# A fused attention and gated-MLP kernel on one core: S2 asked for amid the keys, first keys projected in halves, 256 tokens' features turned by TensorE, batch 0's k v 128 columns wide, steps in a new order

## The chip, the cores and the metric

One core of one Trainium2 chip runs the kernel. The core has five engines with a queue of instructions each: TensorE (PE in the profile, with its weight loads as PEld), VectorE (DVE), ScalarE (ACT), GpSimd (POOL) and SyncE (SP), which here only issues DMAs. An engine takes its instructions in order and waits on semaphores where it needs another's result. The metric is the time of one execution in microseconds; lower is better.

## The reference

Inputs q, k, v have 4 batches, 4 heads, 1088 tokens and 32 dims. Two 8 x 32 sketches S1, S2 give each token 64 features, the products of 8 and 8. The attention is linear: keys and values are summed into a 64 x 32 matrix per head, and each query reads it.

```python
def phi(x):
    a = np.einsum('rd,bhsd->bhsr', S1, x)
    b = np.einsum('rd,bhsd->bhsr', S2, x)
    return np.einsum('bhsi,bhsj->bhsij', a, b).reshape(*x.shape[:-1], r * r)
q_p, k_p = (phi(q), phi(k))
kv = np.einsum('bhsf,bhsd->bhfd', k_p, v)
z = np.sum(k_p, axis=2)
num = np.einsum('bhsf,bhfd->bhsd', q_p, kv)
den = np.einsum('bhsf,bhf->bhs', q_p, z)[..., None] + 1e-06
x = (num / den)            # then 4352 tokens x 128
h = x @ w_in               # 128 x 2048
g = h * (1.0 / (1.0 + np.exp(-beta * h)))
out = g @ w_out            # 2048 x 128
```

## The kernel before

The order of all steps is written out by hand in the string SEQ (L809). Each word of it is a key of the table DO and emits one small step; an engine's queue holds its instructions in the order of these words. Engines run apart from each other and meet on semaphores only.

Per batch, the steps are these. `tk` and `tq` (L433, L439) turn k and q in 32 x 32 blocks on DVE. `kp` (L446) multiplies k by both sketches on PE into a bank `kps`; it has two halves, one for each half of the turned k. `ka` (L464) turns that back into `kab`, the two sets of 8 factors of each token. `o` (L598) forms 64 features `kp` of each key by an outer product, on DVE or POOL, in five parts. `kv` (L627) sums features times v over the nine token groups into the bank `kvz`: for each group and head one product whose weights are 32 columns of v and whose moving operand is 64 features. `gr`, `gc`, `wh`, `wc` (L475 to L505) form from `kab` a small product `wq`, so that the projection of q, step `q` (L510), gives its factors and the summands of its denominator together. `dm`, `di`, `da`, `dx` (L544 to L586) sum the denominator, invert it and scale one factor. `p` (L606) forms q's features `qo`, `t` (L618) turns them in 32 x 32 blocks on DVE into `qt`, `n` (L681) multiplies them by `nd`, a turned copy of `kvz`, with 32 small products for a batch part, and `x` (L698) casts the result into `xT`, 128 features by tokens.

Batch 0 has its queries in two parts: A, the first 256 tokens, and C, the rest. For batch 0, `nd` is made by `ns`, `nt`, `nc` (L642 to L663): a copy of `kvz` repeated four times, two transposes on PE, and a copy. For the other batches `nf` and `ng` (L665, L669) turn it on DVE and pass it through DRAM.

The second half of the work goes over chunks of tokens, 256, 256, seven of 512, and 256. `W` (L395) is a wave: the products of four (or two) of the 16 blocks of w_in with `xT` into a two-bank buffer `wave`, of which there are two, and one Silu on ACT that empties it into `g`. `V` (L424) is a second product of a wave's `g` with the blocks of w_out into the bank `moeout`; after a chunk's last one DVE turns the sum and SP stores it. `kvz` of batch 0 has the bank of the first `moeout`. There are 68 waves and 68 second products.

The weights are prepared on the way. `be` and `bc` (L290, L302) spread beta over the partitions, by PE into a bank and by a copy; `wi` (L308) scales a quarter of w_in by beta; `wa`, `wv`, `wg` (L329, L336) scale one of 16 blocks of w_out by 1/beta on ACT, DVE and POOL. `z0` (L717) writes one element of w_out's tile, so that its load starts only then. `m2` and `ms` (L281, L273) make masked copies of the sketches. Steps `e`, `h`, `i`, `mW` (L248) are filler products on PE with no result.

Loads go through SP's queue, in the order `lk0.0`, `lk0.1` (halves of batch 0's k), `lqA`, `lv0`, `lqC`, the four quarters of w_in, and so on; S1 and beta are issued by ACT, S2 and a second copy of beta by POOL.

## Time and profile before

| | us |
|---|---|
| median of three runs | 102.17 |
| lowest and highest run | 101.83, 102.18 |
| the profiled execution | 100.9 |
| its span, first to last instruction | 99.1 |
| last product on PE ends | 95.2 |
| PE idle from the end of the products to the end of the span | 3.9 |

The profile is one execution. A row of the order-of-time view has the start, the time from the first to the end of the last of the instructions merged into it, the engine, the line, the operation, the tiles, the form and the count; in brackets, the engine's idle time before it and who ended it. A row of the stretches view has, after the stretch and its length, the busy time and count of PE, PEld, DVE, ACT and POOL, then PE's granted clock, the DMA share and GB/s. Busy time of PE counts a product from start to modelled end, so overlapping products make it busy without making it full. The granted clock is 1.00 in the mean of the whole span.

### The profile page before, as it was taken

To read this page: it belongs to the slowest core of one execution; us is meant where nothing else is said; L and a number is where in the kernel's file an instruction comes from. 1 tells how busy PE (TensorE), PEld (TensorE's weight loads), DVE (VectorE), ACT (ScalarE), POOL (GpSimd) and SP (SyncE) were. 2 spreads that over 40 slices of the span, in tenths; PEclk is the share of its full clock that TensorE was granted. 3 is DMA by queue.
4 is the path that set the end of the run, shared out by engine and by line. 5 is a ranking of instruction groups with operands and counts; after the bars stand their busy time and mean duration, and the time that the engine had idled before them with its cause. 6 is when DMAs were issued, how large, how long until landed. Compare 5 with 4: busy or idle time off the path is not lost.

```text
span 99.1 us, 3150 instructions
## 1 busy us (share of the span) xinstructions
PE 92.4 (93%) x1302; PEld 48.7 (49%) x1302; DVE 58.1 (59%) x128; ACT 76.7 (77%) x102; POOL 36.1 (36%) x58
## 2 busy tenths in 40 slices
PE   5989998997999999999999999999999999999940
PEld 2525536665867544434445444444444444446720
DVE  3569989888579998449998335699630020020210
ACT  0505299984869797997998897999989999999910
POOL 5739989998594900077370000320000000000000
PEclk9999999999999999999999999999999999999999
DMA  2999999914971320058043141215015006014163
GB/s 55 273 351 317 395 370 388 270 42 107 387 225 38 62 44 7 0 149 307 17 95 67 20 76 30 53 31 83 2 20 85 1 2 104 7 20 70 17 100 59
DMA packets 24031, 11.75 MB, mean 119 GB/s; under 512 B 19245, under 2 KB 21837, under 8 KB 24017
## 3 DMA queue, kind: packets, MB, share of 16 engines
q1 hardware_dynamic: 23256, 11.44, 41.8%
q8 instruction: 10, 0.16, 0.6%
q10 hardware_dynamic: 696, 0.09, 0.6%
q0 software_dynamic: 64, 0.02, 0.4%
q14 instruction: 5, 0.03, 0.1%
HBM read 9.22 MB, written 2.33 MB: 117 GB/s over the span
## 4 chain that ended last, share of the span: by engine, by line
PE 63%; POOL 12%; ACT 9%; DMA 5%; SPq 4%; issue 2%; DVE 0%; POOLq 0%; ACTq 0%
PE wave L407 27%; PE moeout L379 26%; ACT g L415 8%; DMA w_in_sb<-in_moe_w_in_dram 5%; POOL winp L311 5%; PE nps L689 5%; PE kvz L632 4%; POOL qo L591 3%; POOL kp L591 3%; SPq L143 2%; SPq L164 1%; PE qps L518 1%; ACT xT L705 1%; PE kps L456 1%; SPq L178 1%
## 5 line engine op out<-in xcount | busy, mean ns | idle before, releaser
L415 ACT ACTIVATE g<-wave 128x1024 f16<-128x1024 f32 x68 | 64.8, 1027 | 7.0 <-PE wave L407 6.8
L407 PE MATMUL wave<-xT,winp 128*128 128x512 f16 (+1 forms) x160 | 39.7, 348 | 0.8 <-issue 0.4
L379 PE MATMUL moeout<-g,woutp 128*128 128x512 f16 (+1 forms) x160 | 37.6, 347 | 0.0
L407 PEld LDWEIGHTS <-winp 128*128 128x128 f16 x160 | 17.0, 114 | 16.7 <-issue 6.4
L379 PEld LDWEIGHTS <-woutp 128*128 128x128 f16 x160 | 15.4, 97 | 12.5
L591 POOL TENSOR_TENSOR kp<-kab 128x512 f32<-128x512 f32 (+1 forms) x17 | 16.1, 981 | 10.8 <-DVE kab L465 10.8
L389 DVE STREAM_TRANSPOSE o_sb<-moeout 128x512 f32<-128x512 f32 (+1 forms) x10 | 6.3, 631 | 22.0 <-PE moeout L379 22.0
L622 DVE STREAM_TRANSPOSE qt<-qo 128x512 f32<-128x512 f32 (+1 forms) x21 | 11.8, 605 | 0.2
L591 POOL TENSOR_TENSOR qo<-qa,qab 128x512 f32<-128x512 f32 (+1 forms) x11 | 9.5, 886 | 5.3 <-DVE qa L570 5.3
L535 DVE STREAM_TRANSPOSE qab<-qps 128x576 f32<-128x576 f32 (+2 forms) x10 | 6.0, 642 | 2.1 <-PE qps L518 2.0
L689 PE MATMUL nps<-qt,nd 32*32 32x288 f32 (+2 forms) x320 | 7.0, 364 | 0.1
L253 PE MATMUL kvz<-idle 128*128 128x384 f16 (+1 forms) x21 | 5.1, 399 | 1.1 <-DVE idle L215 1.1
L632 PE MATMUL kvz<-kp,v 128*32 128x64 f32 x288 | 5.7, 222 | 0.3 <-POOL kp L591 0.3
L434 DVE STREAM_TRANSPOSE kT<-k 128x544 f32<-128x544 f32 x8 | 5.6, 719 | 0.4 <-DMA k<-in_k_dram 0.3
L547 POOL TENSOR_TENSOR tmp<-qab 128x64 f32<-128x64 f32 (+2 forms) x3 | 1.8, 589 | 11.0 <-DVE qab L535 11.0
L440 DVE STREAM_TRANSPOSE qT<-q 128x576 f32<-128x576 f32 (+3 forms) x8 | 5.8, 721 | 0.0
L253 PEld LDWEIGHTS <-idle 128*128 128x128 f16 x36 | 3.5, 110 | 4.6 <-issue 2.3
L632 PEld LDWEIGHTS kvz<-kp,v 128*32 128x32 f32 x288 | 4.4, 109 | 2.6 <-issue 1.6
L465 DVE STREAM_TRANSPOSE kab<-kps 128x288 f32<-128x288 f32 x8 | 3.6, 464 | 3.2 <-PE kps L456 3.2
L689 PEld LDWEIGHTS nps<-qt,nd 32*32 32x32 f32 x320 | 3.9, 103 | 2.7 <-DVE qt L622 0.5
L311 POOL TENSOR_TENSOR winp<-w_in_sb,beta_bc 128x512 f16<-128x512 f32 x4 | 5.1, 1274 | 0.1
L332 ACT ACTIVATE woutp<-w_out_sb,rbeta 128x128 f16<-128x128 f32 x15 | 5.0, 399 | 0.1
(63 smaller groups left out, 54.8 us busy)
## 6 DMA issues: line engine op xcount, KB each, us to landing
k<-in_k_dram SPq DMA_DIRECT2D x3, 544.0 KB
q<-in_q_dram SPq DMA_DIRECT2D x3, 544.0 KB, 5.1
v<-in_v_dram SPq DMA_DIRECT2D x4, 288.0 KB
v<-in_v_dram SPq DMA_DIRECT2D x4, 256.0 KB, 5.8
w_in_sb<-in_moe_w_in_dram SPq DMA_DIRECT2D x4, 256.0 KB, 5.4
w_out_sb<-in_moe_w_out_dram SPq DMA_DIRECT2D x4, 256.0 KB, 5.7
out_dram<-o_sb SPq DMA_DIRECT2D x16, 64.0 KB, 3.6
k<-in_k_dram SPq DMA_DIRECT2D x2, 272.0 KB, 2.9
```

Source lines behind the costliest of these rows:

```text
L253: nc.tensor.matmul(out=t[:, P : P + cols], lhsT=idle, rhs=cut(idle, [[0, cols // P], [1, P]]), start=fresh or other, stop=True, skip_group ...
L311: eng.tensor_tensor(out=winp[:, n].rearrange("p c u -> p (c u)"), in0=w_in_sb[:, o : o + FQ], in1=beta_bc[:, o : o + FQ], op=MUL,)
L379: nc.tensor.matmul(out=moe["acc"][:, :tw], lhsT=woutp[:, j // U, j % U, :], rhs=g[jj], start=(j == 0), stop=(j == NJ - 1),)
L389: nc.vector.transpose(out=o_sb[:, :nt, :].rearrange("p t d -> p (t d)"), in_=moe["acc"][:, :tw])
L407: nc.tensor.matmul(out=wv[:, jj // per, o : o + tw], lhsT=winp[:, j // U, :, j % U], rhs=xT[:, t0 : t0 + tw], start=True, stop=True,)
L415: nc.scalar.activation(out=g, in_=wv, func=ACTF.Silu)
L440: nc.vector.transpose(out=qT2[b % 2][:, t0:t1].rearrange("p t s -> p (t s)"), in_=q_t[b][:, t0:t1].rearrange("p t d -> p (t d)"),)
L535: nc.vector.transpose(out=cut(QAB[nm], [[32, 2], [32 * H, n], [1, 32]], 64 * i), in_=PS["qps", nm][i][:, :, : 32 * n],)
L591: eng.tensor_tensor(out=cut(o, [[F, n], [R, R], [1, R]]), in0=cut(a, [[sa, n], [1, R], [0, R]]), in1=cut(b_, [[sb_, n], [0, R], [1, R]]), ...
L622: nc.vector.transpose(out=QT[nm][:, j0:j1].rearrange("p j h c s -> p (j h c s)"), in_=QO[nm][:, j0:j1].rearrange("p j h f -> p (j h f)"),)
L632: nc.tensor.matmul(out=PS["kvz", b][32 * h : 32 * h + 32, :F], lhsT=v_t[b][:, h, j, :], rhs=KP[b][:, j, h, :], start=(j == 0), stop=(j == ...
L689: nc.tensor.matmul(out=t[g // 2][32 * h : 32 * h + 32, g % 2, : 32 * n], lhsT=ND[b][rows, h, fc, :], rhs=QT[nm][rows, :, h, fc, :], start= ...
```

## The change

S2's load is issued by SP (`ls1s`) between the two halves of k, no longer by POOL. The first keys are projected in two halves (`kz0`, `ky0`). Batch 0's `kv` takes, for each of nine groups, two products whose weights are the 128 features of two heads and whose moving operand is 64 columns of v of the same two heads; each sum holds the blocks of both heads with both, of which the equal ones are used. A copy `nn` of 128 columns of it into `ndA` takes the place of `ns`. Part A's features are turned by PE: `TA` makes 128 x 128 transposes, `uA` copies them, and `nA` makes four products of 256 tokens; `xA` copies one block of 128 tokens each. `nd` for part C comes from `nt`, 16 products with slices of the identity, and `nc`. Filler steps `i` are four times three products of 128 columns. Scaling of the second quarter of w_in (`wi1D`) and the product `dmC` go from POOL to DVE, two blocks of w_out (`wg8`, `wg9`) go to POOL, and one beta copy (`bc01D`) to DVE. `store` gets an argument that halves its transfers; it is 0 in every call. SEQ has a new order.

```diff
-    def keep_warm(n, cols, fresh=False, other=False):
-        if other and "warm" not in PS:
-            PS["warm"] = one("warm")
-        t = PS["warm"] if other else kvz0
+    def keep_warm(n, cols, fresh=False, at=P):
         for _ in range(n):
             nc.tensor.matmul(
-                out=t[:, P : P + cols],
+                out=kvz0[:, at : at + cols],
...
         for j in range(j0, j1):
+            if b == 0:
+                for c in range(2):
+                    nc.tensor.matmul(
+                        out=PS["kvz", b][:, F * c : F * c + F],
+                        lhsT=KP[b][:, j, 2 * c : 2 * c + 2, :].rearrange("p h f -> p (h f)"),
+                        rhs=v_t[b][:, 2 * c : 2 * c + 2, j, :],
+                        start=(j == 0 and c == 0),
+                        stop=(j == NJK - 1),
+                        skip_group_check=True,
+                    )
+                continue
...
+    def nd_pairs(copy):
+        t = PS["ndA"] = sbA.tile([P, 2, 2, 32], F32, tag="ndA", name="ndA", bufs=1)
+        copy(out=t.rearrange("p c n d -> p (c n d)"), in_=kvz0[:, :P])
+    def nd_turn():
+        for n in range(4):
+            for g in range(4):
+                nc.tensor.matmul(
+                    out=kvz0[32 * g : 32 * g + 32, P + 64 * n : P + 64 * n + 64],
+                    lhsT=ident[:, 32 * n : 32 * n + 32],
+                    rhs=PS["ndA"][:, :, n // 2, :],
...
+    def turn_a(j):
+        if j == 0:
+            PS["A"] = one("uA")
+            QT["A"] = sbA.tile([P, 2, 2, P], F32, tag="qtA", name="qt", bufs=1)
+        for c in range(2):
             nc.tensor.matmul(
...
+                out=PS["A"][:, 2 * P * j + P * c : 2 * P * j + P * c + P],
+                lhsT=QO["A"][:, j, 2 * c : 2 * c + 2, :].rearrange("p h f -> p (h f)"),
                 rhs=ident,
                 is_transpose=True,
...
+    def copy_a(j, copy):
+        copy(out=QT["A"][:, :, j, :], in_=cut(PS["A"], [[P, 2], [1, P]], 2 * P * j))
+    def num_a():
+        for h in range(H):
+            rows = slice(F * (h % 2), F * (h % 2) + F)
+            nc.tensor.matmul(
+                out=PS["A"][32 * h : 32 * h + 32, : 2 * P],
+                lhsT=PS["ndA"][rows, h // 2, h % 2, :],
+                rhs=QT["A"][rows, h // 2].rearrange("p j s -> p (j s)"),
...
+    def put_xa(i, copy):
+        copy(out=xT[:, P * i : P * i + P], in_=PS["A"][:, P * i : P * i + P])
...
-    DO["i"] = lambda: keep_warm(1, 384, other=True)
+    DO["i"] = lambda: keep_warm(3, P, at=3 * P)
...
-        ls0a ls1g lk0.0s lk0.1s lb4a lbpg m lqAs lv0s lqCs li0s li1s li2s li3s mW h h h h e e tk00 ts msP m2P
-        sq1P sq0P tk01 kp0t ka00 ka01 tqA be00 be01 kx0A bc00A bc01A gr0 gc0D h h wh0 wc0A z0 lo0s lk1s lo1s
-        lo2s lo3s h h qAww o00D rb o01D qtA0 qtA1 tqC lq1s lv1s o04P o02P o03P kv00 i kv01 kv02 i kv03 kv04 ns0A
-        i i i nt0 nc0A dmAP diA daA pA0D tA0 qCwt wi1P pA1P wi0P be10 be11 wa0 wa3 wa1 wa2 bc11A bc10A qtC0 qtC1
-        tA1 dmCP wi3P wi2P tk10 diC tk11 dxC daC pC0D tC0 pC3P pC2P pC1P wa7 wa4 wa5 wa11 i i i i i i i nAww
-        xA1A xA0A wa6 wa14 i i i W W kp1t ka10 ka11 tC3 tC2 tC1 W V gr1 V gc1A wa9 wa8 wa15 W wh1 lk2s tk20 tk21
-        wc1D nCtw xC0A wa12 xC1D tq10 wa13 o10P o11P o12P kv10 kv11 kv12 kp2t ka20 wv10 tq11 ka21 o14P o13P lk3s
...
+        ls0a lk0.0s ls1s lk0.1s lb4a lbpg m lqAs lv0s lqCs li0s li1s li2s li3s mW h h h h e e tk00 ts tk01 tqA
+        m2P msP kz0 ky0 ka00 sq0P ka01 kx0A o00D be00 be01 bc01D o01P o04P o02P gr0 gc0A h h wh0 wc0A z0 lo0s
+        lk1s lo1s lo2s lo3s h h qAtw bc00A qtA0 qtA1 dmAP o03P tqC lq1s lv1s diA daA rb wi1D pA0P pA1P kv00 be10
+        be11 kv01 kv02 qCwt kv03 kv04 qtC0 qtC1 dmCD diC tk10 dxC daC tk11 bc10A bc11A wa1 nn0A wa0 wa2 wi0P
+        pC0D sq1P wi2P pC2P tC0 tC2 pC3P pC1P TA0 TA1 uA0A uA1A i i i i nA wa6 xA1A xA0A wa7 wa4 wa5 nt0 W nc0A
+        wa3 W kp1t W V V ka10 ka11 tC3 tC1 gr1 nCtw tq10 wg9 wi3P wg8 o10P o13P o11P o14P o12P gc1A wa10 wa11
+        wa14 wa15 wa13 xC0A W wh1 wa12 wc1A lk2s tk20 tk21 kp2t xC1D tq11 ka20 ka21 W W lq2s V V q1tw W qt10
+        qt11 kv10 kv11 kv12 kv13 kv14 nf1 dm1P di1 dx1 p10D da1 tq20 ng1s lv2s W W V V W lk3s V V W gr2 W V V W
...
```

Further on in SEQ the same steps of batches 2 and 3 stand in another order: `gr2` after the 11th wave and not the 16th, batch 2's `kv` after the 21st and not the 11th, `gr3` after the 25th and not the 33rd, and the last two parts of batch 3's `kv` after the 35th and not the 30th. From the 36th wave on the order differs by single places of `V` and of steps of DVE and POOL.

More of the change, by code (lines that the diff above doesn't have):

```diff
@@ L350, with store @@
     moe = {"ci": 0, "w": 0, "acc": None, "todo": [], "ready": set()}
-    def store(o_sb, t0, u0, u1, queues):
+    HALVED = 0
+    def store(o_sb, t0, u0, u1, queues, halved=0):
         c = t0 + 32 * u0
@@ L392, in w2 @@
             last = ci == len(tok_chk) - 1
-            store(o_sb, t0, 0, nt, [nc.sync, nc.scalar] if last else [nc.sync])
+            store(o_sb, t0, 0, nt, [nc.sync, nc.scalar] if last else [nc.sync], HALVED if ci == 2 else 0)
     def w1():
@@ L639, in kv, with nd_copy @@
                 )
[L642 to L647 removed]
+    def nd_pairs(copy):
[8 more added lines that the diff above has]
+                    rhs=PS["ndA"][:, :, n // 2, :],
+                    start=True,
+                    stop=True,
+                    skip_group_check=True,
+                )
+    def nd_copy(copy):
+        ND[0] = sbA.tile([P, H, 2, 32], F32, tag="nd", name="nd")
+        copy(
+            out=cut(ND[0], [[32, 4], [128, 2], [1, 32]]),
+            in_=cut(kvz0, [[64, 4], [32, 2], [1, 32]], P),
+        )
+    def turn_a(j):
[3 more added lines that the diff above has]
+        for c in range(2):
             nc.tensor.matmul(
[L649 to L650 removed]
+                out=PS["A"][:, 2 * P * j + P * c : 2 * P * j + P * c + P],
+                lhsT=QO["A"][:, j, 2 * c : 2 * c + 2, :].rearrange("p h f -> p (h f)"),
                 rhs=ident,
@@ L656, in nd_turn @@
             )
-    def nd_copy(b, copy):
-        ND[b] = sbA.tile([P, H, 2, 32], F32, tag="nd", name="nd")
-        copy(
-            out=cut(ND[b], [[32, 2], [64, H], [1, 32]]),
-            in_=cut(PS["kvz", b], [[P, 2], [32, H], [1, 32]], P),
-        )
+    def copy_a(j, copy):
[7 more added lines that the diff above has]
+                rhs=QT["A"][rows, h // 2].rearrange("p j s -> p (j s)"),
+                start=True,
+                stop=True,
+                skip_group_check=True,
+            )
+    def put_xa(i, copy):
+        copy(out=xT[:, P * i : P * i + P], in_=PS["A"][:, P * i : P * i + P])
+        moe["ready"].update(range(4 * i, 4 * i + 4))
     def nd_flip(b):
@@ L758 @@
             DO[f"lq{nm}{c}"] = lambda r=r, qu=qu: load_rows(q, q_t, 0, qu, r)
+    DO["nt0"] = nd_turn
+    DO["nA"] = num_a
+    for c in "AD":
+        DO["nn0" + c] = lambda c=c: nd_pairs(COPY[c])
+        DO["nc0" + c] = lambda c=c: nd_copy(COPY[c])
+        for n in range(2):
+            DO[f"uA{n}{c}"] = lambda n=n, c=c: copy_a(n, COPY[c])
+    for n in range(2):
+        DO[f"TA{n}"] = lambda n=n: turn_a(n)
     JR = {b: [(0, 2), (2, 4), (4, 5), (5, 7), (7, 9)] for b in range(B)}
```

51 lines of the change are left out of this document (23 added, 28 removed).

## The prediction

> **What bounds the kernel now.** I read the page first, then the stretches, then the first 28 us in order of time. The page gives the span, each engine's busy time and the chain that ended last.
>
> ```profile
> span 99.1 us, 3150 instructions
> PE 92.4 (93%) x1302; PEld 48.7 (49%) x1302; DVE 58.1 (59%) x128; ACT 76.7 (77%) x102; POOL 36.1 (36%) x58
> PE 63%; POOL 12%; ACT 9%; DMA 5%; SPq 4%; issue 2%; DVE 0%; POOLq 0%; ACTq 0%
> ```
>
> The chain is not one thing: its DMA, POOL and SP shares come first, its PE share after. The stretches show the same by stage.
>
> ```profile
> 10.00:16.60 6.60, 6.37 (x172) 3.27 (x161) 5.98 (x15) 4.59 (x15) 6.12 (x7) 1.00 1.02 385
> 16.60:24.40 7.80, 6.98 (x186) 4.68 (x186) 6.83 (x14) 6.38 (x13) 7.80 (x9) 1.00 0.52 151
> 28.00:40.00 12.00, 11.96 (x210) 7.03 (x204) 10.86 (x20) 9.48 (x12) 5.58 (x7) 1.00 0.26 58
> 72.00:95.20 23.20, 23.19 (x178) 12.20 (x146) 2.93 (x5) 21.31 (x23) 0.00 (x0) 1.00 0.23 38
> ```
>
> From 28 us on PE has 0.04 us without work in 12, later 0.01 in 23. All that follows is the same list of waves and second products before and after the change, so a delay at 28 us has nothing to disappear into, and a lead is kept. The change is decided by how far the kernel is at 28 us. Three marks lead there.
>
> ```profile
> 8.81 0.41 PE L518 MATMUL qps<-qT,wq 32*32 32x64 f32 x32
> 16.64 1.03 PE L407 MATMUL wave<-xT,winp 128*128 128x256 f16 x8 [0.27 <-ACT xT L705]
> 17.28 2.85 ACT L415 ACTIVATE g<-wave 128x1024 f16<-128x1024 f32 x3
> 27.27 0.78 PE L518 MATMUL qps<-qT,wq 32*32 32x288 f32 x32
> ```
>
> These are the first q projection, the first wave, the first Silu, and q of batch 1, whose end at 28.05 is my third mark. By then seven waves, four second products and all of batch 1's k v are done.
>
> **S2 and the halved keys.** Today S2 is asked for by POOL. Now SP issues it between the two halves of k.
>
> ```profile
> 0.74 0.88 SPq L143 DMA_DIRECT2D k<-in_k_dram  x2
> 0.74 0.68 ACTq L116 DMA_DIRECT2D sr<-in_S_dram  x1
> 4.53 0.24 DVE L269 STREAM_TRANSPOSE st<-sr 128x64 f32<-128x64 f32 x1 [0.23 <-DMA sr<-in_S_dram]
> 4.70 0.70 DVE L434 STREAM_TRANSPOSE kT<-k 128x544 f32<-128x544 f32 x1
> 4.86 0.25 POOL L274 TENSOR_TENSOR sk<-st,hm 128x32 f32<-128x32 f32 x1 [0.67 <-DVE st L269]
> 5.55 0.72 PE L456 MATMUL kps<-kT,sk 64*32 64x288 f32 x16 [0.39 <-POOL s2bd L282]
> 6.36 0.85 DVE L465 STREAM_TRANSPOSE kab<-kps 128x288 f32<-128x288 f32 x2 [0.96 <-PE kps L456]
> 7.13 0.40 DVE L440 STREAM_TRANSPOSE qT<-q 128x256 f32<-128x256 f32 x1
> ```
>
> DVE waits for S2 until 4.53, and the projection starts at 5.55, after the second turned half of k. S2 on SP should land some 0.5 us sooner, and the first half is projected while DVE turns the second. Against this, the issue of S2 (0.68 us as S1 on ACT) stands ahead of k's second half and of every later load, and qT is now turned ahead of kab, so kab waits for q too. Bounds for kab: 0.5 us sooner (what the wait gives) to 0.2 later (0.68 less the slack of k's second half). I take 0.25 sooner. The projection of q then starts at 8.5, since the beta copies no longer stand on ACT ahead of wq.
>
> **k v of batch 0, 128 wide.** 36 products of 32 columns become 18 of 128. Each float32 product is two passes. The old ones ran four side by side in column groups. The new ones fill the array, one at a time, and load four times the columns per pass.
>
> ```profile
> 9.15 0.43 PE L632 MATMUL kvz<-kp,v 128*32 128x64 f32 x16
> 31.66 1.14 PE kvz L632 x72
> L294 PEld LDWEIGHTS betaps<-beta,ones x8: 181/182/184, 6.2 to 12.7; 1*128 1x128 f32 x8
> 6.20 0.30 PEld L294 LDWEIGHTS betaps<-beta,ones 1*128 1x128 f32 x4 [0.47 <-issue]
> L648 PEld LDWEIGHTS kvz<-ident,kvd x2: 138/140/143, 11.7 to 11.7; 128*128 128x128 f32 x2
> 11.66 0.20 PEld L648 LDWEIGHTS kvz<-ident,kvd 128*128 128x128 f32 x2 [0.28 <-ACT kvd L644]
> ```
>
> The cost of a batch today is 1.14 us for 72 passes. No row shows a 128-column float32 product of this kind, so I bound its weight load. Four loads for the beta products, each 182 ns, end 0.30 us after the first began: the last pair began 0.30 - 0.18 = 0.12 us after the first, so a load takes about 0.11. The two transposes' loads of 140 ns fit in 0.20: 0.06 us apart. The weights of k v are an ordinary float32 operand, as beta's are, so I take 0.11; the stream of 64 columns (0.055 us: the old passes, four abreast, 1.14 / 72 = 0.016 each, with their issue) hides under it. 36 x 0.11 = 3.9 us against 1.14: 2.8 more. Low end 36 x 0.06 = 2.2 us; high end with load and stream in turn, 36 x 0.165 = 5.9.
>
> The Trainium skill, page "TensorE: Matmul & The Clock Gate", section "LDWEIGHTS (loading the stationary operand)", counts columns divided by 1.2 in ns, and its next section keeps the fast load from float32. That is an estimate of 107 ns for 128 columns, 3.8 us in all, and speaks against the low end; the beta row agrees, the transposes' row does not.
>
> **Up to the first wave.** What else stands on PE in that order, and on ACT behind it:
>
> ```profile
> 12.03 0.66 PE L518 MATMUL qps<-qT,wq 32*32 32x224 f32 x32
> 12.62 1.13 PE L294 MATMUL betaps<-beta,ones 1*128 1x512 f32 x4
> 11.67 0.44 PE L648 MATMUL kvz<-ident,kvd 128*128 128x128 f32 x2
> 13.68 1.31 PE L253 MATMUL warm<-idle 128*128 128x384 f16 x7
> 14.93 0.85 PE L689 MATMUL nps<-qt,nd 32*32 32x64 f32 x64
> 11.24 0.37 ACT L644 COPY kvd<-kvz 128x256 f32<-128x256 f32 x1 [2.51 <-PE kvz L632]
> 16.19 0.41 ACT L705 CAST xT<-nps 128x128 f16<-128x128 f32 x2
> 20.07 1.01 ACT L332 ACTIVATE woutp<-w_out_sb,rbeta 128x128 f16<-128x128 f32 x3
> 7.79 0.68 DVE L591 TENSOR_TENSOR kp<-kps,kab 128x512 f32<-128x512 f32 x1
> 10.39 1.28 POOL L311 TENSOR_TENSOR winp<-w_in_sb,beta_bc 128x512 f16<-128x512 f32 x1
> 14.01 0.66 POOL L547 TENSOR_TENSOR tmp<-qab 128x224 f32<-128x224 f32 x1 [0.34 <-DVE qab L535]
> ```
>
> Today k v ends at 11.2 and 13 fillers follow (0.16 us each, 7 in 1.31), so PE has room before the first wave. The new order uses it up: q of A 8.5 to 8.85; k v's first 8 passes to 9.75; the beta products, which need their copy's bank, to 10.8; 12 passes to 12.1; q of C to 12.75; 16 passes to 14.5; with 0.1 us at each of four changes of tile form, 14.9. Two things wait behind that. ACT then copies the k v pairs (0.25, of 0.37 for twice the columns) and, in its order, two scaled blocks of w_out (0.34 each): 16.0. Two copies of the turned features (0.37 each): 16.75. Four products of 256 columns, four abreast, 0.6 (bounds 0.44 and 0.85): 17.4. The copies of xT 0.41 and their hand-over: first wave at 17.9, 1.3 us later than today. The four transposes (0.11 each) are hidden under ACT's copies; without that cover they cost 0.45. The removed fillers, spread and two 0.37 copies save nothing here, for they were in the room. winp's second quarter on DVE (bounds 0.68 and 1.28 us, DVE's and POOL's price for that size; I take 0.7) ends by 12.5, hidden under k v; C's product for its sums, now on DVE too (some 0.66), is hidden until C's own features are wanted, and pushes those.
>
> **From the first wave to the third mark.** ACT has three more blocks of w_out ahead of its first Silu (1.0): first Silu at 18.9 against 17.28. Then up to the fifth Silu stand five of them (0.95 each), seven w_out blocks (2.35), and the copies of nd 0.37, of gsb, of x of C and of wq, some 0.85 together: 8.3, to 27.3. q of batch 1 needs the wave bank that this Silu frees, 0.75; a wave 0.43; k v of batch 1, which used to be half done, 1.14, and 0.15 of changes: 29.8. POOL must not be later than that:
>
> ```profile
> 20.01 0.20 ACT L491 COPY gsb<-gram 128x32 f32<-128x32 f32 x1
> 22.32 0.48 ACT L705 CAST xT<-nps 128x384 f16<-128x384 f32 x1 [0.32 <-PE nps L689]
> 17.09 2.68 POOL L591 TENSOR_TENSOR qo<-qa,qab 128x256 f32<-128x256 f32 x3
> 19.73 4.74 POOL L591 TENSOR_TENSOR kp<-kab 128x512 f32<-128x512 f32 x5
> ```
>
> Today its k features of batch 1 end at 24.47. Now C's three features begin near 17.2 (2.7), winp's last quarter follows (1.3), two w_out blocks (0.34 as on ACT) and the five k features (4.7): 26.6, ahead of PE's need at 28.5. So 1.75 us late at the mark (k v 1.3 of it at the first wave, ACT's order the rest).
>
> **Afterwards.** The second half of the order moves gram and k v of batches 2 and 3 by a few steps; each has the same instructions, and qt of batch 1, the tightest, is ready near n1's turn as today. I count -0.4 to +0.4, middle -0.1. The stores and tail are the same (the new argument of store is 0 in every call). Sum: +1.65, from 99.1 to 100.75 of span. The profiled execution took 100.9 outside, 1.8 over its span, and the median of the three runs 102.17, 1.27 above it; the prediction is set on the median: 102.17 + 1.65 = 103.8. Its own range, from the bounds: 102.7 to 105.2.
>
> **Rivals.**
> - Faster. The k v load has the transposes' price, 0.06, taking 1.8 off the head, and kab gains its whole 0.5: first wave near 15.8, 0.85 ahead. ACT then has its three blocks done by 16.9, its Silus 0.4 ahead, and the later order keeps that and gains 0.2: -0.6, 101.6. For it speaks the transposes' row; against it beta's. It decides below 0.07 us a pass.
> - Even. Cheap loads as above but ACT's w_out blocks eat the lead: fifth Silu at 25.9, mark at 28.2: +0.1, 102.3. ACT's 7.80 us stretch after the first wave, with 6.38 busy, has only 1.4 to spare for such shifts.
> - Worse. S2's 0.68 on SP delays v, C's q and w_in as well, for DMA is busy 1.02 of its time in the first stretch quoted and can't catch up; C's q (DVE turns it ahead of A's sums) then holds back A's features and C's whole row by 0.7: +0.9 more, 104.7.
> - The halves give nothing, because the second half still waits for the second half of k: +0.25, inside the range.
>
> **Numbers.** Forecast 0.47 (103.8), worse 0.14 (104.7), even 0.16 (102.3), faster 0.23 (101.6). Half a per cent, about what a measurement can tell from no change, is 0.5 us. So slower 0.61, same 0.16, faster 0.23. The range goes from 101.3 to 105.2; it leaves out the lower part of the faster case and 0.05 above.
>
> **What would show it.** k v of batch 0: 36 passes 0.11 us apart and PEld rows near 180 ns (0.06 and 140: the first two rivals). The first wave near 17.9; the first Silu near 18.9 with three w_out blocks ahead of it; q of batch 1 ending after 28.2. kab starting near 6.1 shows the S2 part. Wrong if the first wave comes before 16.6, or if the stretches after 28 us show PE with gaps that the delay could fill.

## The result, and the profile after

The changed kernel is slower: 1.029 times the time before (95% interval 1.0245 to 1.0337). Two of its four executions took 104.97 and 104.94 us, beside a median of 102.0 (101.77 to 102.18) for the kernel before on the same chip; the other two, at 106.91 and 231.44, count as disturbed and are left out. The profiled execution took 104.97, its span is 103.2. The span before was 99.1, so the two profiles differ by 4.1 us, where the prediction had 1.65. The times differ by less, 2.95 us (104.95 against 102.0), because the profiled execution before was, at 100.9, 1.1 us under its kernel's median.

The page of the changed kernel: the span, each engine's busy time, the clock's line of 40 slices (2.6 us each, tenths of full speed) and the chain that ended last.

```profile
span 103.2 us, 3056 instructions
PE 97.4 (94%) x1257; PEld 54.2 (53%) x1257; DVE 58.4 (57%) x127; ACT 76.7 (74%) x103; POOL 35.1 (34%) x57
PEclk9999955699999999999999999999999999999997
PE 89%; ACT 6%; DVE 1%; issue 0%
```

PE has 5.0 us more to do than before (97.4 against 92.4) with 45 instructions fewer, and the chain is now almost PE alone (89%, before 63%). The clock's line shows why at a glance: three slices, from 13 to 20 us, at 5 to 6 tenths. Before, all forty read 9. The stretches view of PE by itself, cut where the clock changes, has the start and end, PE's busy time and count, the granted clock, the DMA share and GB/s:

```profile
6.15:9.57 3.42, 3.42 (x100) 1.00 0.98 304
9.57:12.98 3.41, 3.41 (x36) 1.00 1.00 349
12.98:16.39 3.41, 3.41 (x45) 0.50 1.03 401
16.39:19.80 3.41, 3.41 (x24) 0.50 0.75 283
19.80:23.20 3.40, 3.29 (x70) 1.00 0.53 169
```

For 6.83 us PE ran at half speed. PE was not idle before that: the second row has 3.41 busy of 3.41. What it did in that row, and after, stands in the order of time of PE:

```profile
6.17 0.72 PE L458 MATMUL kps<-kT,sk 64*32 64x144 f32 x32
9.24 0.39 PE L520 MATMUL qps<-qT,wq 32*32 32x64 f32 x32
9.56 1.11 PE L636 MATMUL kvz<-v,kp 128*128 128x64 f32 x8
10.60 1.13 PE L291 MATMUL betaps<-beta,ones 1*128 1x512 f32 x4
11.66 1.65 PE L636 MATMUL kvz<-v,kp 128*128 128x64 f32 x12
13.24 1.05 PE L520 MATMUL qps<-qT,wq 32*32 32x224 f32 x32
14.21 3.67 PE L636 MATMUL kvz<-v,kp 128*128 128x64 f32 x16
17.68 1.06 PE L685 MATMUL uA<-ident,qo 128*128 128x128 f32 x4
18.53 1.44 PE L250 MATMUL kvz<-idle 128*128 128x128 f16 x12
21.09 1.04 PE L409 MATMUL wave<-xT,winp 128*128 128x256 f16 x8
```

Within a group the passes of k v come about 0.11 us apart until the clock falls; the last 16, in the slow stretch, come at 0.22 (3.47 us to the next row). The projection of C's q takes 1.05 where it took 0.66. The first wave starts at 21.09, before at 16.64: 4.45 later. Behind it nothing is lost: span minus first wave is 82.1 here and 82.5 before, and from 28 us on PE is as full as it was.

```profile
28.00:40.00 12.00, 11.98 (x194) 7.94 (x186) 9.72 (x21) 10.13 (x13) 5.05 (x6) 1.00 0.49 134
72.00:95.00 23.00, 23.00 (x164) 10.92 (x163) 4.91 (x8) 21.49 (x25) 0.00 (x0) 1.00 0.27 45
```

So the head, the work ahead of the first wave, holds all of it. At its start stands a second, smaller delay. SP's issues and DVE's rows in order of time:

```profile
1.18 0.69 SPq L116 DMA_DIRECT2D sr<-in_S_dram  x1
1.92 0.57 SPq L143 DMA_DIRECT2D k<-in_k_dram  x1
4.42 0.24 DVE L266 STREAM_TRANSPOSE st<-sr 128x64 f32<-128x64 f32 x1 [0.23 <-DMA sr<-in_S_dram]
5.55 0.74 DVE L436 STREAM_TRANSPOSE kT<-k 128x544 f32<-128x544 f32 x1 [0.88 <-DMA k<-in_k_dram]
6.99 0.85 DVE L467 STREAM_TRANSPOSE kab<-kps 128x288 f32<-128x288 f32 x2 [0.37 <-PE kps L458]
```

S2 is there only 0.11 us sooner than before (4.42 against 4.53), but DVE now waits 0.88 us for the second half of k, which SP issues behind S2. The turn of that half starts at 5.55 (before 4.70), `kab` at 6.99 (before 6.36).

This pair of profiles makes the second delay look surer than it is. PE opens every execution with 17 filler products and can't start on the keys before they are through. Here are 12 of them in the kernel before, the same 12 in the changed kernel, 14 in e8 (an experiment below whose head is the old one, unchanged), and e8's `kab`:

```profile
2.64 2.52 PE L253 MATMUL kvz<-idle 128*128 128x384 f16 x12
2.62 3.62 PE L250 MATMUL kvz<-idle 128*128 128x384 f16 x12
1.99 4.26 PE L253 MATMUL kvz<-idle 128*128 128x384 f16 x14
7.01 0.85 DVE L465 STREAM_TRANSPOSE kab<-kps 128x288 f32<-128x288 f32 x2 [1.22 <-PE kps L456]
```

At first the fillers start 0.32 us apart, later 0.15 to 0.16. In the kernel before the pace doubles at 3.9 us, in e4 (the old head too) at 5.0; in the changed kernel and in e8 all 17 go at the slow pace, up to 6.2. I read this as PE at half clock until then, although the clock column reads 1.00 for the whole of it. With the late opening the old head has `kab` at 7.01 and the first wave at 17.23, not at 6.36 and 16.64. So some 0.6 us of the 4.45 can come from the moment at which the fast pace sets in, which differs between executions of one and the same head, and not from the change.

### The profile page after: what moved, and what is told of

It reads as the page before. It is cut to its first block, busy times and chain, and to the rows that moved or that the text cites. A ratio compares the mean times of both kernels' runs of the same rounds, so it can differ in the third digit from the quotient of the medians.

```text
span 103.2 us, 3056 instructions
## 1 busy us (share of the span) xinstructions
PE 97.4 (94%) x1257; PEld 54.2 (53%) x1257; DVE 58.4 (57%) x127; ACT 76.7 (74%) x103; POOL 35.1 (34%) x57
## 4 chain that ended last, share of the span: by engine, by line
PE 89%; ACT 6%; DVE 1%; issue 0%
PE wave L409 29%; PE moeout L381 28%; PE kvz L250 7%; PE kvz L636 6%; PE nps L739 5%; PE kvz L646 3%; PE qps L520 3%; ACT woutp L329 3%; PE betaps L291 2%; PE kps L458 2%; ACT g L417 2%; PE gram L481 1%; PE uA L685 1%; PE uA L701 1%; PE gram L497 1%; DVE o_sb L391 0%
## 5 line engine op out<-in xcount | busy, mean ns | idle before, releaser
L409 PEld LDWEIGHTS <-winp 128*128 128x128 f16 x160 | 16.6, 115 | 16.8 <-issue 6.3
L593 POOL TENSOR_TENSOR kp<-kab 128x512 f32<-128x512 f32 (+1 forms) x15 | 14.6, 997 | 11.1 <-DVE kab L467 11.1
L593 POOL TENSOR_TENSOR qo<-qa,qab 128x512 f32<-128x512 f32 (+1 forms) x13 | 11.4, 900 | 18.1 <-DVE qa L572 18.1
L624 DVE STREAM_TRANSPOSE qt<-qo 128x512 f32<-128x512 f32 (+1 forms) x19 | 11.0, 626 | 0.1
L250 PE MATMUL kvz<-idle 128*128 128x384 f16 (+1 forms) x33 | 7.6, 409 | 1.0 <-DVE idle L215 1.0
L636 PEld LDWEIGHTS kvz<-v,kp 128*128 128x128 f32 x36 | 5.9, 255 | 1.5 <-POOL tmp L549 0.8
L636 PE MATMUL kvz<-v,kp 128*128 128x64 f32 x36 | 6.4, 347 | 0.0
L739 PE MATMUL nps<-qt,nd 32*32 32x288 f32 (+1 forms) x256 | 6.2, 399 | 0.1
L755 DVE CAST xT<-nps 128x512 f16<-128x512 f32 (+2 forms) x4 | 2.8, 691 | 4.1 <-PE nps L739 4.0
L593 DVE TENSOR_TENSOR qo<-qps,qab 128x512 f32<-128x512 f32 x7 | 4.7, 667 | 0.1
L739 PEld LDWEIGHTS nps<-qt,nd 32*32 32x32 f32 x256 | 3.3, 103 | 2.3 <-ACT g L417 1.4
```

Source lines behind the costliest of these rows:

```text
L250: nc.tensor.matmul(out=kvz0[:, at : at + cols], lhsT=idle, rhs=cut(idle, [[0, cols // P], [1, P]]), start=fresh, stop=True, skip_group_che ...
L409: nc.tensor.matmul(out=wv[:, jj // per, o : o + tw], lhsT=winp[:, j // U, :, j % U], rhs=xT[:, t0 : t0 + tw], start=True, stop=True,)
L593: eng.tensor_tensor(out=cut(o, [[F, n], [R, R], [1, R]]), in0=cut(a, [[sa, n], [1, R], [0, R]]), in1=cut(b_, [[sb_, n], [0, R], [1, R]]), ...
L624: nc.vector.transpose(out=QT[nm][:, j0:j1].rearrange("p j h c s -> p (j h c s)"), in_=QO[nm][:, j0:j1].rearrange("p j h f -> p (j h f)"),)
L636: nc.tensor.matmul(out=PS["kvz", b][:, F * c : F * c + F], lhsT=KP[b][:, j, 2 * c : 2 * c + 2, :].rearrange("p h f -> p (h f)"), rhs=v_t[b ...
L739: nc.tensor.matmul(out=t[g // 2][32 * h : 32 * h + 32, g % 2, : 32 * n], lhsT=ND[b][rows, h, fc, :], rhs=QT[nm][rows, :, h, fc, :], start= ...
```

## The experiments

Twelve kernels ran. "Ratio" is to the kernel before on the same chip, with its 95% interval; first wave, span and clock are those of each one's profiled execution. The diffs are shortened, and `...` stands for what is left out.

| kernel | first wave | span | clock | median us | ratio |
|---|---|---|---|---|---|
| before | 16.64 | 99.1 | 1.00 | 102.0 | 1 |
| changed | 21.09 | 103.2 | 0.96 | 104.95 | 1.029 (1.025 to 1.034) |
| e1, fillers in k v | 24.97 | 107.4 | 0.95 | 109.64 | 1.074 (1.065 to 1.083) |
| e2, k v in column groups | 21.02 | 102.9 | 0.97 | 104.95 | 1.032 (1.024 to 1.040) |
| e3, S2 on POOL | 22.11 | 104.3 | 0.95 | 106.2 | 1.043 (1.037 to 1.048) |
| e4, before without 5 fillers | 16.91 | 99.5 | 1.00 | 101.72 | 0.998 (0.991 to 1.005) |
| e5, 256 columns streamed | 22.31 | 104.5 | 1.00 | 106.37 | 1.044 (1.040 to 1.049) |
| e6, narrow k v | | | | 104.41 | 1.014 (1.008 to 1.020) |
| e7, narrow, S2 on POOL | 17.45 | 102.0 | 1.00 | 103.65 | 1.018 (1.013 to 1.023) |
| e8, old head, new order | 17.23 | 100.7 | 1.00 | 102.44 | 0.998 (0.993 to 1.003) |
| e9, new head, old order | 17.13 | 102.3 | 1.00 | 103.75 | 1.018 (1.010 to 1.027) |
| e10, 128 columns streamed | 18.46 | 100.5 | 0.99 | 102.72 | 1.008 (1.004 to 1.012) |
| e11, e10 and S2 on POOL | 18.12 | 100.7 | 1.00 | 102.37 | 1.004 (1.001 to 1.007) |
| e12, e11 and keys whole | 18.14 | 101.5 | 0.99 | 103.35 | 1.014 (1.011 to 1.017) |

(The changed kernel's 104.95 lies between its 104.94 and 104.97. Clocks of 0.99 have no stretch of 0.50 before the last products.)

### The clock, first try: fillers, column groups, and the old kernel without fillers

Three theories on the half clock: it came from the wide passes, from the fillers that no longer stand between the parts of k v, or by chance. The first kernel puts fillers back.

```diff
-... kv00 be10 be11 kv01 kv02 qCwt kv03 kv04 ...
+... kv00 i be10 i be11 i kv01 i kv02 i qCwt i kv03 i kv04 ...
```

> Changed kernel with seven more filler steps (21 products of 128 columns whose result nobody reads, about 1.2 us of PE work at full clock) spread between the parts of batch 0's k v, the beta products and q of C. Theory A (the PE clock was halved from 12.98 to 19.80 us because k v as wide passes, without the old fillers between its parts, leaves the array too little active): granted clock 1.00 in both stretches 10.00:16.60 and 16.60:24.40, the last 16 k v passes take 1.8 us instead of 3.6, first wave near 19 instead of 21.09, median 1 to 2 us below the changed kernel's 104.95 although PE got more work. Theory B (the passes themselves and the order cost the time, the clock drop is chance or comes from something else): clock still 0.5 somewhere in the head, or the time is 0.5 to 1.2 us above 104.95.

It came out worse than either theory had it: 109.64. The stretches of PE in e1, cut at the clock's changes:

```profile
11.43:14.84 3.41, 3.41 (x24) 1.00 1.04 391
14.84:18.25 3.41, 3.41 (x49) 0.50 1.04 400
18.25:21.67 3.42, 3.42 (x20) 0.50 0.14 49
21.67:25.08 3.41, 3.41 (x54) 0.50 0.50 167
```

The clock fell all the same, and stayed down for three such stretches instead of two. (The third is not the fillers' doing by itself: e3, below, has no added fillers and three as well.) So small fillers among the passes do not hold it. That speaks against "the missing fillers"; it does not say what does.

The second kernel cuts the width: each product in four of 32 feature columns, side by side.

```diff
-    out=kvz[:, F*c : F*c+F],
-    lhsT=KP[b][:, j, 2*c : 2*c+2, :]
+  for g in range(4):
+    h, f = 2*c + g//2, 32 * (g % 2)
+    out=kvz[32*g : 32*g+32, F*c : F*c+F],
+    lhsT=KP[b][:, j, h, f : f+32],
...
```

> Changed kernel with only the width undone: every k v product of batch 0 cut into four of 32 feature columns, side by side in column groups, with the same result (72 products instead of 18). From the old k v row, 1.14/72 = 0.016 us per pass, 144 passes give 2.3 us, against 36 passes at 0.11 = 3.9 at full clock and 6.2 as measured. Theory A (wide form with its long weight loads starves the clock): clock 1.00 throughout or a drop that comes later, k v 2.3 us, first wave near 17 to 18, time 101.5 to 102.7. Theory A2 (the missing fillers alone starve it, whatever the form): clock still halves, time 103 to 105. Theory B (order and S2 are what costs): time stays above 103.5 with clock 1.00.

The passes were cheaper, and the clock fell again, later, and most likely for another reason. PE in order of time, and in stretches:

```profile
12.27 0.63 PE L520 MATMUL qps<-qT,wq 32*32 32x224 f32 x23
14.38 0.58 PE L520 MATMUL qps<-qT,wq 32*32 32x224 f32 x9 [1.48 <-issue]
...
12.25:15.66 3.41, 1.93 (x95) 1.00 1.03 384
15.66:19.07 3.41, 3.41 (x48) 0.50 0.93 352
```

In the middle of C's projection PE stood for 1.48 us and waited for nothing that the profile shows. The same view of the DMA queues, for 11.9 to 13.1 us, shows one transfer of another kind among the loads:

```profile
q8 instruction: 1, 0.02, 4.9%
```

It is 16 KB of instructions, over by 13.1, and PE went on at 14.38. This form sends more instructions through PE than the changed kernel (1365 products in all against 1257), all of the surplus before that point or soon behind it. That PE had run out of fetched instructions is the reading I take; no experiment isolates it. The same run has a second such stand, of 0.91 us before 20.85, with one such transfer between 18.3 and 19.5; but the changed kernel has ten of these transfers too, as many as e2, and no such stand. With both stands in its head, e2 does not price the narrow form. For the clock the run decides nothing, since PE was busy 1.93 us of 3.41.

The fourth kernel takes five fillers out of the kernel before.

```diff
-... kv00 i kv01 kv02 i kv03 kv04 ns0A i i i nt0 ...
+... kv00 kv01 kv02 kv03 kv04 ns0A nt0 ...
```

> Kernel before without the five fillers amid and right behind batch 0's k v (narrow passes, four abreast). Theory A (wide passes starve the clock): clock stays 1.00 and the time within 0.5 us of 102.0. Theory A2 (fillers alone hold the clock): the clock halves for 6.8 us around 11 to 18 us and the time rises by 1.5 to 3 us.

The clock column reads 1.00 throughout, and the time is unchanged. One stretch of it:

```profile
10.00:16.60 6.60, 5.65 (x147) 2.92 (x145) 5.98 (x14) 4.30 (x14) 6.19 (x8) 1.00 1.02 393
```

PE was idle for 0.95 us of these 6.6 and kept its clock, while the changed kernel, never idle, lost it. Busy time, as the profile counts it, is not what the clock goes by. The narrow passes also need no fillers among them.

### The clock, second try: the same passes with a longer stream

A wide pass waits for its 128 columns of weights (0.11 us) and then streams 64 columns. A filler of 384 columns takes 0.16 us (row in the prediction), 0.42 ns a column. If float32 columns stream at the same rate, 64 columns are an estimated 0.027 us: a quarter of the pass. If the clock goes by how long columns stream, streaming more behind the same weights must hold it. Nothing else is changed: same products, same weights, same order. The columns that are added are not used, and the copy `nn` picks out the blocks that are.

```diff
-    out=kvz[:, F*c : F*c+F],
-    rhs=v_t[b][:, 2*c : 2*c+2, j, :],
+    out=kvz[:, 256*c : 256*c+256],
+    rhs=cut(v_t[b], [[0, 2], [NJK*D, H], [1, D]], D*j),
...
```

> Changed kernel with the same 18 wide k v products, the same weights in the same order, but each streams 256 columns of v (all heads, twice over) instead of 64; only 64 columns of each are used after it. 256 columns take 0.11 us by the beta row (512 columns, 4 passes in 0.85 us of stream), as long as the load of 128 weight columns, so at full clock a pass should stay near 0.11 to 0.13 us although four times as much goes through the array. Theory A' (the clock goes by how long columns stream through the array, and passes that wait for their weights leave it too little; fillers of 0.16 us each were too few): clock 1.00 from the head on, 16 last passes in 1.8 to 2.1 us instead of 3.6, first wave near 18, time 102.3 to 103.5. Theory A'' (the clock falls with wide float32 passes as such, or by power): clock still halves, 16 passes 3.6 us or more, time 105 to 107.

The clock was held, and the price was not the one expected. PE in order of time in e5, and its stretch:

```profile
15.92 3.72 PE L636 MATMUL kvz<-v,kp 128*128 128x256 f32 x16
22.31 1.04 PE L409 MATMUL wave<-xT,winp 128*128 128x256 f16 x8
...
10.00:16.60 6.60, 6.60 (x59) 4.39 (x58) 2.94 (x9) 1.54 (x4) 6.11 (x9) 1.00 1.04 384
```

A pass of 256 columns takes 0.22 us at full clock (3.56 to the next row, by 16): about what a load (0.11) and a stream of 256 columns (0.11 by the estimate above) take one after the other, not hiding each other. So e5 is slower than the changed kernel in spite of its clock. It does settle that wide float32 passes as such do not pull the clock down.

With 128 columns (each head of v once) both come together.

```diff
-    out=kvz[:, F*c : F*c+F],
-    rhs=v_t[b][:, 2*c : 2*c+2, j, :],
+    out=kvz[:, P*c : P*c+P],
+    rhs=v_t[b][:, :, j, :],
...
```

> As e5_stream, but 128 columns of v (all heads, once) streamed behind each load of 128 weight columns, twice what the changed kernel streams; half of the result is not used. A pass took 0.11 us with 64 columns and 0.235 with 256 at full clock, so 128 should take 0.11 to 0.155: 4.0 to 5.6 us for the 36 passes, against 6.2 as they ran in the changed kernel, half of them at half clock. Theory A' (the clock goes by how long columns stream; 24% of a pass in the changed kernel, where it fell, 45% in e5, where it held; here some 35 to 48%): if that is enough, clock 1.00, first wave 18.7 to 20.0, span 100.8 to 102.2, time 102.6 to 104.0, so less time for twice the stream. If it isn't enough: clock 0.5 for 6.8 us or more, first wave past 21, time 105 to 107. If the head is not what holds the end (the order behind it is): time stays at 104.5 to 105.5 though the clock is held and the first wave comes before 20.

PE in order of time in e10, and its stretches:

```profile
9.50 1.13 PE L636 MATMUL kvz<-v,kp 128*128 128x128 f32 x8
11.62 1.60 PE L636 MATMUL kvz<-v,kp 128*128 128x128 f32 x12
13.74 2.05 PE L636 MATMUL kvz<-v,kp 128*128 128x128 f32 x16
18.46 1.03 PE L409 MATMUL wave<-xT,winp 128*128 128x256 f16 x8
...
10.00:16.60 6.60, 6.60 (x83) 5.15 (x82) 5.03 (x13) 2.33 (x8) 6.07 (x8) 1.00 1.03 394
16.60:24.40 7.80, 6.95 (x169) 4.47 (x166) 7.40 (x15) 7.27 (x21) 7.08 (x9) 1.00 0.51 187
```

Twice the stream in the same products, and the kernel is 2.2 us faster (102.72 against 104.95). The last 16 passes take 1.89 us to the next row, 0.118 each, where they took 3.47. The first wave comes 2.63 sooner and the span is 2.7 shorter. Chance does not explain it. Of the 28 executions of the three kernels that stream 128 columns (e10, e11, e12), 27 had a mean clock of 0.988 or more and one 0.975; the eleven executions of the changed kernel, e1 and e3, leaving out that of 231.44 us, had 0.938 to 0.968. So the half clock costs 2.2 us by the medians and 2.7 by the two profiles, and it comes when the wide passes stream little: more stream behind the same weights, alone, holds the clock.

How the clock's measure weighs work stays open. The border lies somewhere between an estimated 24% of a pass (64 columns) and 45% (0.053 of 0.118), if it is a matter of the pass alone. A plain count of streamed columns it is not likely to be: in the stretch ahead of its fall e1 had nine fillers of 128 columns and some 10 passes of 64, by columns about as much as e10's passes in a stretch (some 13 of 128), and it fell. And in the changed kernel, e1 and e3 the stretch ahead of the fall also holds beta products, which use one row of the array; no experiment takes them out.

### S2 and the halved keys

First in the changed kernel itself:

```diff
-ls0a lk0.0s ls1s lk0.1s ...
+ls0a ls1g lk0.0s lk0.1s ...
```

> Changed kernel with S2 asked for by POOL again, ahead of k, so that SP's next loads are issued 0.7 us sooner; keys still in halves. Theory C (S2's issue on SP delays the second half of k, and so kab by 0.6 us, and with it all of the head): kab near 6.2 instead of 6.99, first wave 0.5 to 0.7 sooner, and 0.4 to 0.7 us off 104.95, unless the clock windows move against it. Rival (k's second half lands late because the DMAs are full): kab stays after 6.8 and the time within 0.3 of 104.95.

`kab` started at 6.51 instead of 6.99, and the time rose to 106.2: everything up to the second group of k v came 0.5 us sooner (11.17 against 11.66), but the clock fell there and stayed low longer. Its mean was 0.63 in the stretch from 10.00 to 16.60 and 0.66 from 16.60 to 24.40, against 0.73 and 0.79. With the clock unsettled, half a microsecond at the start can't be read from the time. So it was repeated on e10, with the same edit:

> The kernel of e10_stream128 (clock held, 102.72 us) with S2 asked for by POOL ahead of k, as in the kernel before; keys still in halves. Theory C (S2's 0.69 us of issue on SP made k's second half land at 5.5 instead of 4.3 us): DVE turns the second half near 5.0 instead of 5.52, kab at 6.4 to 6.6 instead of 6.90, first wave 0.3 to 0.5 sooner (18.0 to 18.2), time 102.2 to 102.5. Rival (the head has another bound by then, POOL's features or ACT's blocks of w_out): kab sooner, but the first wave within 0.2 of 18.46 and the time within 0.2 of 102.7.

DVE and PE in order of time in e11:

```profile
5.18 0.74 DVE L436 STREAM_TRANSPOSE kT<-k 128x544 f32<-128x544 f32 x1
6.56 0.85 DVE L467 STREAM_TRANSPOSE kab<-kps 128x288 f32<-128x288 f32 x2 [0.31 <-PE kps L458]
18.12 1.03 PE L409 MATMUL wave<-xT,winp 128*128 128x256 f16 x8
```

As expected: no wait for k, `kab` and the first wave 0.34 us sooner than in e10 (6.90 and 18.46), the median 0.35 lower. That S2 on SP costs 0.35 us is the best guess, but not shown: the two kernels ran on different chips, and their ratios, 1.008 (1.004 to 1.012) and 1.004 (1.001 to 1.007), overlap.

What stands firm is the place. In the six kernels with S2 on SP, `st` starts at 4.01 to 4.42 and the turn of k's second half at 5.52 to 5.82; in the eight with S2 on POOL these are 4.50 to 4.92 and 4.66 to 5.18. `kab` starts at 6.90 to 7.20 in the six. In the eight it starts at 6.36 to 6.57 where the opening fillers are done by 5.7 us, and at 6.79 to 7.10 in the three (e7, e8, e9) where they are not. Last, the keys in one piece again:

```diff
-... tk00 ts tk01 tqA m2P msP kz0 ky0 ka00 sq0P ka01 ... pC0D sq1P wi2P ...
+... tk00 ts msP m2P sq1P sq0P tk01 kp0t ka00 ka01 tqA ... pC0D wi2P ...
```

> The kernel of e11_s128_s2pool with the first keys projected in one piece again, in the kernel before's order of steps up to there: the whole S2 and keys part undone. Theory F (halving the projection gives nothing, for the second half still waits for the second half of k, and it puts qT ahead of kab): kab at 6.3 to 6.4 as in the kernel before, time within 0.3 of e11. Theory of the prediction (halves give 0.25): kab 0.1 to 0.3 later than in e11, time 0.1 to 0.3 above it.

`kab` starts at 6.57, the first wave at 18.14: to 0.02 us what the halves gave. In these two executions the halves give nothing. The time is 1.0 us higher, though, and not in the head:

```profile
56.80 1.59 PE L739 MATMUL nps<-qt,nd 32*32 32x288 f32 x64 [1.09 <-DMA nd<-ndw]
```

Batch 2's `nd` came late from its way through DRAM, and PE stood for it 1.09 us.

### The order of the steps, and the narrow k v

Can the new way for part A be had without wide passes? In the next two kernels v is the weight again (32 columns, four abreast) and 128 features of a pair stream; one copy and one transpose give the same paired layout.

```diff
-    out=kvz[:, F*c : F*c+F], lhsT=KP pair, rhs=v pair
+    out=kvz[32*h : 32*h+32, :P], lhsT=v_t[b][:, h, j, :], rhs=KP pair
...
-... kv03 kv04 ... nn0A ... TA0 TA1 ...
+... kv03 kv04 ... kc0A TA0 TA1 kt0 nn0A ...
```

> Changed kernel with batch 0's k v products turned round: v of a head as 32 columns of weights, four abreast, the pair's 128 k features streamed; one ACT copy and one transpose by TensorE then give the same paired layout as before. Loads fall from 36 x 128 to 72 x 32 columns in four groups; by the old row (1.14 us for 72 passes of 64 columns) 72 passes of 128 take 1.2 to 1.6 us instead of 6.2 as measured and 3.9 at full clock; the copy and the transpose add some 0.7. Theory A': clock 1.00, first wave near 16.6 to 17.2, time 101 to 102.3. Theory D (fetching of PE's instructions stalls it, as between 12.9 and 14.4 us of the kernel with four column groups, where more instructions went through PE before 13 us): a gap of more than 1 us without a releaser on PE in the head, time over 103.

> The kernel of e6_narrow with S2 asked for by POOL again. Theory C (S2 on SP delays the keys' second half by 0.6 us): kab 0.5 to 0.6 sooner than in e6_narrow, the first wave 0.3 to 0.6 sooner, time 0.3 to 0.6 below it. Rival: loads on SP land no sooner, or PE waits for its instructions or for POOL's features instead: within 0.25.

e6 took 1.014 times the time before, outside its expected 101 to 102.3. Its profiled execution took 105.27, its shortest 103.04, so nothing rests on its rows; they have a stand of 1.00 us with no releaser, much as the second theory had it. e7 missed as well: `kab` is 0.20 us sooner than in e6 (6.79 against 6.99), not 0.5 to 0.6, since the opening fillers end at 6.0 there, and its times (103.14 to 104.19) are not below e6's shorter two (103.04 and 103.56). In e7 the clock is held and the first wave comes at 17.45, a little behind the 16.6 to 17.2 expected of this form, yet the span is 102.0. PE in order of time has the reason:

```profile
37.51 1.59 PE L755 MATMUL nps<-qt,nd 32*32 32x288 f32 x64 [0.82 <-DMA nd<-ndw]
```

and another 1.04 us at batch 2's product. That led to a theory that the new order leaves `nd` no slack, and to two kernels that cross the heads and the orders: e8 has the old kernel's steps up to `o12P` and then the new order, e9 the head of e7, with blocks of w_out moved behind the first wave and nine of twelve fillers left out, and then the old order.

```diff
-... wa13 o10P o11P o12P kv10 kv11 kv12 kp2t ka20 ...
+... wa13 o10P o11P o12P o14P o13P kp2t tq11 wv10 ka20 ka21 W W lq2s V V q1tw W qt10 qt11 kv10 ...
```

> Kernel before with its own head up to the x copies of C (PE near 22 us), followed by the changed kernel's order of steps (k v of batch 1 behind q of batch 1, its bounce nd through DRAM and the loads and stores as there). Theory E (the new order leaves the nd bounce no slack, so that a head that is not late makes PE wait: 1.9 us of waits for nd were seen with the first wave at 17.45 and 0.82 to 1.04 at each of n1 and n2): first wave near 16.6, PE waits for nd at n1 and n2, 1.5 to 2.6 us in all, span 100.8 to 101.8, time 1.5 to 2.5 us above the kernel before. Theory of the prediction (the order behind 28 us is worth -0.4 to +0.4): no wait over 0.3 us, time within 0.5 of the kernel before.

```diff
-... kc0A TA0 TA1 kt0 nn0A wa1 wa0 wa2 ... uA0A uA1A i i i i nA wa6 xA1A xA0A wa7 wa4 wa5 nt0 W nc0A wa3 W ...
+... kc0A wa1 TA0 TA1 kt0 nn0A uA0A uA1A wa0 wa2 ... i nA xA1A xA0A wa3 nt0 W nc0A wa6 W kp1t wa7 wa4 W wa5 ...
```

> The kernel of e7_narrow_s2 (narrow k v, one transpose, S2 on POOL) with ACT's scaled blocks of w_out moved behind what the first wave needs and 11 of 12 fillers before A's products gone; from k's next batch on the old order of steps. Theory E: PE has no wait for nd over 0.3 us behind 28 us, and span minus first wave is near 82.5 (84.5 in e7). First wave at 16.5 to 17.0 by the sum of e7's rows (A's products can follow the copies of its features, which follow ndA: 16.27 less 1.0 of w_out blocks, less 0.1), span 99 to 99.6, time 101.8 to 102.6, about that of the kernel before. Rival (the head's own work, POOL or ACT, is late in both orders): span minus first wave stays over 84, time over 103.

The theory is not borne out in its size. e8's ratio is 0.998 (0.993 to 1.003), and over all ten of its executions the mean is 0.2 us above that of the kernel before, give or take 0.5; 1.5 to 2.5 were expected. But the wait is there, once. At batch 2's product e8 stands as e7 and e12 do:

```profile
55.93 1.59 PE L689 MATMUL nps<-qt,nd 32*32 32x288 f32 x64 [1.11 <-ACT g L415]
```

The profile puts this down to a Silu that ended at that moment. But in e10 the same product starts at 55.65, before the Silu of the same wave begins (55.77), so it does not need that Silu, and most likely waits in e8 for `nd` too. e8's span less first wave is 83.5, 1.0 more than before. e9 missed as well, by waits of its own making. PE's waits in e9, in total, times, longest:

```profile
PE moeout L381 <- ACT woutp L329: 1.4, 2, 0.9
PE kps L458 <- DVE qo L593: 0.5, 1, 0.5
```

Blocks of w_out that no longer stand ahead of the first Silu are missing at the second products. The wait at batch 2's product thus comes in some profiles of this order (e7, e12 and most likely e8) and not in others (the changed kernel, e10, e11). In the first three SP issues `nd`'s load 4.9 to 5.1 us behind the issue of the write that it reads back, in the others 3.8 to 4.5. What delays it was not tried.

No kernel here beats the one before beyond what can be measured; e4 and e8 are level with it.

## Why the prediction was right or wrong

The direction was right, and the 104.95 measured lies 1.15 us above the forecast of 103.8, inside the range. That it lies inside is in part luck. The range was built without the clock, which alone cost 2.2 to 2.7 us. And the forecast added its span of +1.65 to a median 1.27 above the profiled execution, so a span that grew by 4.1 became a time that grew by 2.95. The rival at 104.7 came nearest to the number, by delays of v and C's q that are not what cost the time.

- **S2 and the halved keys: wrong.** The step gave `kab` 0.25 us sooner, with 0.2 later as the worse bound. It came 0.63 later. "0.68 less the slack of k's second half" took slack for granted: the turn of that half began at 4.70 before, directly behind `st`, and with S2 ahead of it in SP's queue it lands so late that DVE waits 0.88 us. S2 itself gained only 0.11 in this pair; over all kernels `st` starts 0.1 to 0.9 sooner with S2 on SP, so the forecast 0.5 was fair. What it costs at the end is not settled (0.35 by e11, with overlapping intervals), and where the opening fillers end late it costs `kab` nothing (7.01 in e8, 6.99 here). The small rival "the halves give nothing" was right in e12's pair, and the larger one, that S2's issue delays what SP loads behind it, had the right queue, but at k instead of v and C's q.
- **k v at 0.11 us a pass: right.** 9.56 to 10.60 for eight, with a change of form in it, and loads of 186 to 193 ns. The Trainium skill's count (page "TensorE: Matmul & The Clock Gate", section "LDWEIGHTS (loading the stationary operand)") agrees with these rows. The price holds at full clock only. The 0.055 us for the stream, which set the high end, has no row: the old passes give 4 x 0.016 = 0.063 with their issue, the fillers' rate an estimate of 0.027.
- **Up to the first wave: this step failed.** It added rows of the kernel before, all taken at a granted clock of 1.00, and set the first wave at 17.9; it came at 21.09. The 16 last passes were to take 1.75 us and took 3.47, C's projection 0.65 and took 0.97 to the next row, and the transposes and fillers that followed ran at half speed too. The clock was no term of the sum, no bound and no rival. (A slip beside that is small: 14.9 + 0.25 + 0.68 is 15.83, not 16.0.) With the clock held and everything else as in the change (e10), the first wave comes at 18.46, 0.56 behind the forecast, which S2's misjudged part more than covers.
- **From the first wave to the third mark: right, at full clock.** Forecast: fifth Silu done at 27.3, k v of batch 1 done at 29.8. In e10 it is 27.0 (26.07 and half of two in 1.94) and 29.80. The agreement is of two errors: e10's first wave is 0.56 late and this stage 0.56 short, 11.34 us against 11.9. In the changed kernel k v of batch 1 ends at 32.42, 11.33 behind its first wave. The three blocks of w_out stand ahead of the first Silu as said.
- **Afterwards: right for this kernel.** A delay at 28 us is kept to the end. Span less first wave is 82.1 after and 82.5 before, inside the -0.4 to +0.4 us allowed. The order does not always keep to that: in e7, e8 and e12 PE stands 1.0 to 1.1 us at batch 2's product.
- **The sum.** +1.65 of span was forecast; e10's profile, with the clock held, has +1.4, and its median +0.75 over the kernel before on its chip. Both profiled executions are short ones of their kernels, the one before more so. The changed kernel has +4.1 of span, of which 2.7 is the half clock. The mechanism of the forecast (wide k v, ACT's blocks, a list that keeps every delay) was right as far as it went, and the term that was mis-sized is PE's time in the head: 1.3 us later forecast, 4.45 measured.

On the clock the Trainium skill, page "TensorE: Matmul & The Clock Gate", section "What's actually happening", tells of a free-running window of 3413 ns and a half clock after an idle one. The length agrees: the slow stretches are two and three times 3.41 us. The condition doesn't: the window ahead of the fall was busy 3.41 of 3.41.

## What to carry to other kernels

Price a rearranged product by its weight loads, and then ask what share of its time anything streams: passes that wait for 128 float32 columns and stream 64 can cost themselves and their neighbours half the clock although PE looks fully busy. Read the granted clock in the stretches before durations are carried from one kernel to another, and the pace of the first products too: one and the same head reached its first wave at 16.64, 16.91 and 17.23 (before, e4, e8). A load put in front of another in an issuing queue takes its issue time from everything behind it, so look first whether the next one has any slack.

## What the runs showed of the hardware that was not expected

- The granted clock fell to 0.50 for 6.83 us with PE busy throughout (changed kernel), and stayed at 1.00 with 0.95 us idle in 6.6 (e4).
- Behind a float32 load of 128 columns, 64 and 128 streamed columns cost nearly the same, about 0.11 and 0.118 us a pass, but 256 cost 0.22. What sets in between 128 and 256 is not known.
- Fillers of 128 columns between such passes did not hold the clock: it was low for 10.2 us (e1), and for 10.2 without them (e3).
- The first fillers of an execution start 0.32 us apart and later ones 0.15 to 0.16, and for the same head the change comes at 3.9, 5.0 and not before 6.2 us (before, e4, e8). The clock column does not show it.
- PE can stand 1.48 us for no releaser that the profile names, near a 16 KB transfer of the instruction queue (e2); that the one causes the other is not shown.
